# Attention and a spectral filter on one core: how score tiles, fold sums and fillers are planned, and where loads and stores stand

## The chip, the cores and the metric

The kernel runs on one core of a Trainium2 chip. The metric is the device time of one execution in microseconds. Five engines work side by side, each through its own instruction stream: TensorE (PE), VectorE (DVE), ScalarE (ACT), GpSimd (POOL) and SyncE (SP, which only issues transfers here). They wait for each other by semaphores.

## The reference

Two independent results stand side by side in the output, each 2048 x 448:

```
qkv = (x @ wqkv) -> 3 x 16 heads x 2048 x 28
p   = softmax(q k^T / sqrt(28));   a = (p v) @ wo
X   = rfft2(B_x) * (w_r + i w_i);  b = irfft2(X)
out = concat([a, b], -1)
```

The left half is full attention with 16 heads of 28 columns. The right half multiplies a two-dimensional real Fourier transform by given weights and transforms back. All inputs and the output are bf16.

## The kernel before

**Attention.** The 16 heads are four groups (`NG`) of four heads, which share the four row or column quarters of the TensorE array. A *block* is one group with 512 queries: 16 blocks. A block has 16 key chunks of 128 keys. A *unit* is the score tile of one head for one key chunk and 512 queries; there are 16 x 16 x 4 = 1024. A *fill* (`fill`, line 897 on) multiplies up to four units of different heads at once into PSUM banks (line 905). Units go one of two ways. Those of ScalarE are exponentiated in one instruction for one, two or three banks (line 934) into `ET`, which has `ESL = 16` slots. Those of VectorE (key chunks `DKS = (3, 7, 11)`) take a cheaper form: one pass reads the bank, adds a bias and writes 16-bit integers (line 944), whose bits are read as bf16; three shifted copies follow (line 949), and each copy is multiplied by values scaled beforehand (`Vs`, line 516). The four together make a good exponential. The value products (line 1001) of one block add up in one fixed bank, number 6, one step for a ScalarE chunk and four for a VectorE chunk. When the block is closed, `finish` copies the bank out (line 1060), brings the sums of the softmax to lanes with a small product, takes the reciprocal, spreads it with a second product and multiplies on VectorE (line 1058).

**Spectral half.** Rows are folded into even and odd sums (`fold_chunk`, two chunks on VectorE and two on GpSimd, all operations recorded by `tt`, line 546), then come `s_job` and `x_job` (transforms as products with tables), `zmul` (sixteen small operations per tile on GpSimd), `i_job` (back), `combine` (GpSimd) and 16 `y_job` output products. The weights arrive by 16 plain loads and 16 gathers.

**Order.** All streams are written out ahead by a planner in Python with its own clock (`Prog`, and the main loop at the end). ScalarE is served first: a fill is emitted `TH` before ScalarE runs out. Value products, projections and spectral jobs fill the rest in the order of due times (`due`), counted in ScalarE units done. Every instruction has a price; a step of a job is priced by the job's width, even where its product is narrower. Where the plan leaves TensorE idle for more than `FGAP` and its recent activity is below `FACT = 0.95`, a filler is emitted: matmuls of constants into a free bank (line 1333), whose results are not read. VectorE and GpSimd operations that use the port to the on-chip memory that these two share carry `port=True`: such an operation waits for the other engine's last one, so they take turns. Transfers are issued mostly by SyncE, in program order; a transfer's wait holds all transfers behind it.

**Ends.** At the start all of A's input is loaded at once, 20 warm-up matmuls run (line 1089), weights are spread into padded copies (line 424), and the first keys and queries are projected. At the end each output tile goes through one of four staging slots (`astg`) to one store by SyncE (line 761).

Of the kernel before, what the change touches and what calls it, by code (L numbers as in the profile page):

```python
# [13 lines left out]
TAIL = {"pe": 0.28, "act": 0.34, "dve": 0.14, "pool": 0.12, "sp": 0.1}  # L14
# [7 lines left out]
class Prog:  # L22

    def __init__(self, nc, sems):
# [14 lines left out]
        self.port = (None, None, 0.0)  # L39
        self.hist = {e: {} for e in ENG}  # L40
# [51 lines left out]
    def ready(self, eng, reads=(), writes=()):  # L92
        t = 0.0
        for k in list(reads) + list(writes):
            w = self.tw.get(k)
            if w is not None and not (eng == "pe" and w[0] == "pe"):
                t = max(t, w[1])
        for k in writes:
            for r, e in self.tr.get(k, {}).items():
                if r != eng:  # L100
                    t = max(t, e)
        return t
# [19 lines left out]
    def dma(self, eng, fn, sem, reads=(), writes=(), kb=128, issue=0.6):  # L122
        assert not self.blocked((), writes), (eng, reads, writes)
        self._emit_waits(eng, reads, writes)
# [4 lines left out]
        start = max(self.free[eng], self.ready("dma", reads, writes))  # L129
        self.free[eng] = start + issue  # L130
        self.dma_free = max(self.dma_free, start + issue) + kb / 220.0
        self._mark("dma", ev, reads, writes, self.dma_free + 2.0)
# [45 lines left out]
    def flush(self, now):  # L178
        nxt = INF
        again = True  # L180
        while again:
            again = False
            nxt = INF
            for eng in ("dve", "pool"):
# [5 lines left out]
                for n in self.queue[eng]:  # L190
# [45 lines left out]
def spectral_constants():  # L236

    i = np.arange(512)
    even = 2 * np.pi * ((i[:, None] * i[None, :]) % 1024) / 1024
    odd = np.pi * ((i[:, None] * (2 * i[None, :] + 1)) % 2048) / 1024  # L240
# [3 lines left out]
    fo[1, 0, :] = -((-1.0) ** i)  # L244
    tab = np.stack([fe, fo, go]).reshape(3, 2, 4, 128, 512).transpose(0, 3, 1, 2, 4)
    alt = np.zeros((128, 512))
    alt[0] = (-1.0) ** i
    vec = np.zeros((128, 6))
    a = (-1.0) ** np.arange(128)
    vec[:, 0], vec[:, 1], vec[:, 2], vec[:, 3], vec[:, 4], vec[:, 5] = a, a, -a, a, a, -a  # L250
# [5 lines left out]
    t1 = np.zeros((128, 2, 2, KD))  # L256
    for b, m in enumerate((c[0:113], c[113:225], sn[1:113], sn[113:224])):
        t1[0:m.shape[0], b // 2, b % 2] = m
    dd = np.arange(D)
# [12 lines left out]
DKS = (3, 7, 11)  # L272
ND = len(DKS)
ESL = 16
TSL = 8
# [3 lines left out]
FILLER, FGAP, FACT = True, 0.15, 0.95  # L279
DBL, NDF = 2.5, 1  # L280
PH = ((0.10, 0.30), (0.31, 0.44), (0.58, 0.76), (0.78, 0.985))
FOLD = ((0, "pool"), (1, "dve"), (2, "pool"), (3, "dve"))
# [14 lines left out]
def build_kernel(nc, A_x, A_wqkv, A_wo, B_x, B_w_r, B_w_i, out):  # L297
    WARM = 20
# [13 lines left out]
    t1_h = nc.inline_tensor(t1.reshape(128, 4 * KD).astype(bf16np), name="cst_t1")  # L312
    t2_h = nc.inline_tensor(t2.reshape(128, 4 * D).astype(bf16np), name="cst_t2")
    pp = np.arange(128)
    idx = np.zeros((128, 16), np.int32)
    for a in range(2):
        for c in range(4):
            idx[:, 4 * a + c] = np.minimum(1024 * (a + 1) - 128 * c - pp, S - 1)
    for t in range(8):
        idx[:, 8 + t] = np.minimum(2048 - (t // 4) - 256 * (t % 4) - 2 * pp, S - 1)  # L320
    idx[0, 8] = 1024
# [4 lines left out]
    with ctx:  # L326
        sem_names = ["pe", "act", "dve", "pool"]
        sem_names += ["d_x%d" % i for i in range(4)] + ["d_w", "d_wv", "d_wo", "d_c", "d_t", "d_xe"]
        sem_names += ["d_i"] + ["d_xr%d" % i for i in range(4)] + ["d_wr%d" % i for i in range(8)]
        sem_names += ["d_xb%d" % i for i in range(4)] + ["d_f%d" % i for i in range(2)] + ["d_wb%d" % i for i in range(8)] + ["d_o%d" % i for i in range(4)]  # L330
# [7 lines left out]
        wq = sb("wq", [128, 4, NG, 128])  # L338
        wk = sb("wk", [128, 4, NG, 128])
        wo = sb("wo", [128, NG, 448])  # L340
# [3 lines left out]
        Vs = sb("Vs", [128, 2, ND, NW - 1, 128])  # L344
        ET = sb("ET", [128, ESL, 512])
        TT = sb("TT", [128, NW, TSL, 512], I16)
# [3 lines left out]
        cid = sb("cid", [128, 260])  # L350
        R1a = sb("R1a", [128, 7200])
        R1b = sb("R1b", [128, 7616])
        R2 = sb("R2", [128, 8192])
        FR = sb("FR", [128, 2, 4096])
        alt_t = sb("alt", [128, 518])
        T1 = sb("T1", [128, 2, 2, KD])
        T2 = sb("T2", [128, 2, 2, D])
        ptmp = sb("ptmp", [128, 1800], F32)
        idx_t = sb("idx", [128, 16], mybir.dt.int32)
        ext = sb("ext", [128, 2, KD])  # L360
        PS = ctx.enter_context(nc.psum_tensor("PS", [128, 4096], F32))
        ACC = PS[:, 3072:3584]

        wflat = wst[:, :, :].rearrange("p c k -> p (c k)")
        astg = wflat[:, 0:1792].rearrange("p (s d) -> p s d", s=4)
        xB = R1a[:, :].rearrange("p (a c d) -> p a c d", a=4, c=4)
        XZ = R1a[:, :].rearrange("p (t v k) -> p t v k", t=8, v=4)
        fA = R1b[:, 0:7168].rearrange("p (a c d) -> p a c d", a=4, c=4)
        xtra = R1b[:, 7168:7616]
        Wn = R1b[:, 0:7200].rearrange("p (t v k) -> p t v k", t=8, v=4)  # L370
# [3 lines left out]
        Sd = R2[:, :].rearrange("p (b r k) -> p b r k", b=4, r=2)  # L374
# [3 lines left out]
        vec_r = alt_t[:, 512:518].rearrange("p (v k) -> p v k", v=3)  # L378
        onf = onrm[:, :, :].rearrange("p g k -> p (g k)").bitcast(F32)
        LD = onf[:, 1024:3712].rearrange("p (a d) -> p a d", a=6)  # L380
        L0 = {"dve": LD[:, 0:4], "pool": ptmp[:, 0:1792].rearrange("p (a d) -> p a d", a=4)}
# [200 lines left out]
        def s_job(h, r, b, due):  # L582
# [16 lines left out]
            def after():  # L599
                done.add(("s", h, r, b))  # L600
                if all(x in done for x in alls):
                    load_f(2, 1)
                    for t in range(8):
                        load_w(t)
# [792 lines left out]
```

## Time and profile before

| what | value |
|---|---|
| median of 3 runs | 468.45 us (467.98 to 470.62) |
| span of the profiled execution | 460.5 us |
| the median beyond that span | 7.95 us |
| PE busy | 424.8 us, 92% |
| ACT busy | 395.2 us, 86% |
| DVE busy | 348.2 us, 76% |
| POOL busy | 165.5 us, 36% |
| mean granted TensorE clock | 0.978 |

The profile is of one execution and gives its span, from the first instruction to the last; its own device time is not given beside it, so the difference of the median to the span is what lies around. Busy shares are averages over parts with different limits, so the table by stage is the one to read. PEclk is the granted share of TensorE's full clock.

### The profile page before, as it was taken

The page shows a single profiled execution, that of the slowest core. Times are in us where ns is not written, and L with a number is a line of the kernel's source. Part 1 is how long each engine was busy: PE and PEld are TensorE (multiplying, and loading weights), DVE is VectorE, ACT ScalarE, POOL GpSimd, SP SyncE. Part 2 cuts the span into 40 slices and gives each one's busy share as a digit, 9 for nine tenths or more (in the row PEclk, how much of TensorE's full clock was granted, in tenths as well). Part 3 has the DMA queues.
Part 4 walks back from the last instruction along what each step waited for, and adds up shares of the span by engine and source line. Part 5 has one row for each costly group of instructions (what it writes and reads, how often), then busy time and mean ns, then how long its engine had stood idle before and what let it go on. Part 6 is the DMA issues. An engine that isn't in the chain of part 4 may idle for free.

```text
span 460.5 us, 16944 instructions
## 1 busy us (share of the span) xinstructions
PE 424.8 (92%) x7484; PEld 164.9 (36%) x7484; DVE 348.2 (76%) x731; ACT 395.2 (86%) x383; POOL 165.5 (36%) x203
## 2 busy tenths in 40 slices
PE   7889899988998899998998899999899999999994
PEld 3434433332332233433333333333332332423353
DVE  2856699999989397676768788968668788996361
ACT  2687569999999899995899999999999999999911
POOL 8775700000000000686376566465652335320000
PEclk9999999999999899995899999999999999999998
DMA  8940000000000000720000000000000000011132
GB/s 237 333 152 4 3 2 3 1 4 1 3 1 2 1 4 1 210 48 1 2 3 3 2 3 3 2 3 3 1 3 1 4 1 2 3 33 41 62 113 83
DMA packets 13421, 15.92 MB, mean 35 GB/s; under 512 B 3762, under 2 KB 12212, under 8 KB 12964
## 3 DMA queue, kind: packets, MB, share of 16 engines
q1 hardware_dynamic: 11332, 11.39, 8.0%
q0 software_dynamic: 1088, 2.24, 1.8%
q10 hardware_dynamic: 928, 1.20, 0.9%
q8 instruction: 59, 0.97, 0.9%
q14 instruction: 14, 0.11, 0.1%
HBM read 11.16 MB, written 3.67 MB: 32 GB/s over the span
## 4 chain that ended last, share of the span: by engine, by line
PE 41%; ACT 23%; DVE 16%; POOL 8%; DMA 6%; issue 6%; SPq 0%; DVEq 0%; ACTq 0%; POOLq 0%
ACT ET L934 22%; PE PS L443 13%; PE PS L1001 13%; PE PS L905 13%; DVE TT L944 5%; DVE TT L949 4%; POOL R1b L541 3%; DMA out_dram<-wst 2%; DMA R1a<-in_B_x_dram,idx 2%; DVE onrm L546 2%; PE PS L1333 2%; DMA wst<-in_A_wqkv_dram 2%; POOL ptmp L546 1%; POOL R1b L546 1%; POOL wst L546 1%
## 5 line engine op out<-in xcount | busy, mean ns | idle before, releaser
L934 ACT ACTIVATE ET<-PS 128x1024 bf16<-128x1024 f32 (+2 forms) x373 | 388.6, 1153 | 35.4 <-PE PS L905 33.1
L905 PE MATMUL PS<-qT,kT 28*128 28x512 bf16 x1024 | 149.4, 390 | 13.6 <-ACT ET L934 8.9
L944 DVE TENSOR_SCALAR TT<-PS 128x512 int16<-128x512 f32 x192 | 129.5, 685 | 32.8 <-PE PS L905 31.0
L949 DVE TENSOR_SCALAR TT<-TT 128x1024 int16<-128x1024 int16 x288 | 105.9, 421 | 12.8 <-POOL ptmp L546 11.5
L1001 PE MATMUL PS<-ET,Vaug 128*32 128x512 bf16 x832 | 83.4, 394 | 4.4 <-ACT ET L934 3.6
L905 PEld LDWEIGHTS PS<-qT,kT 28*128 28x128 bf16 x1024 | 36.6, 91 | 120.4 <-ACT ET L934 66.3
L1333 PE MATMUL PS<-cid 128*32 128x256 bf16 x1216 | 56.0, 275 | 3.6 <-DVE qT L495 1.3
L541 POOL DMA_INDIRECT R1b<-in_B_w_r_dram,idx x8 | 8.0, 998 | 130.0 <-DVE R L607 127.9
L1001 PE MATMUL PS<-TT,Vs 128*32 128x512 bf16 x576 | 40.3, 384 | 0.1
L1001 PEld LDWEIGHTS PS<-ET,Vaug 128*32 128x32 bf16 x832 | 21.2, 94 | 48.6 <-issue 32.1
L546 POOL TENSOR_TENSOR ptmp<-ptmp,R1b 128x450 f32<-128x450 f32 x32 | 31.6, 1010 | 14.1 <-DVE TT L949 10.0
L1333 PEld LDWEIGHTS PS<-cid 128*32 128x32 bf16 x1216 | 27.1, 95 | 26.7 <-issue 7.7
L546 POOL TENSOR_TENSOR R<-R1b 113x512 bf16<-113x512 f32 (+3 forms) x16 | 20.0, 1276 | 36.3 <-DVE R1b L707 33.8
L546 POOL TENSOR_TENSOR ptmp<-R1a 128x225 f32<-128x225 bf16 (+2 forms) x36 | 25.1, 716 | 15.7 <-DVE TT L949 12.8
L443 PE MATMUL PS<-T,R 112*32 112x448 bf16 (+4 forms) x512 | 28.0, 323 | 2.1 <-DVE TT L944 1.8
L546 POOL TENSOR_TENSOR ptmp<-ptmp 128x225 f32<-128x225 f32 x32 | 18.1, 582 | 17.2 <-DVE TT L949 9.2
L546 POOL TENSOR_TENSOR R1a<-ptmp 128x225 bf16<-128x225 f32 x32 | 18.0, 581 | 12.7 <-DVE TT L949 11.7
L443 PE MATMUL PS<-FR,R1b 128*32 128x512 bf16 (+3 forms) x256 | 21.6, 397 | 0.8 <-ACT ET L934 0.6
L443 PE MATMUL PS<-FR,R1a 128*32 128x512 bf16 (+2 forms) x256 | 21.1, 383 | 0.3
L1001 PEld LDWEIGHTS PS<-TT,Vs 128*32 128x32 bf16 x576 | 15.4, 98 | 14.6 <-DVE TT L949 1.0
L443 PE MATMUL PS<-wv,xAT 112*32 112x112 bf16 x1024 | 20.5, 219 | 0.0
L443 PE MATMUL PS<-xAT,wk 112*32 112x512 bf16 x240 | 19.2, 382 | 0.9 <-DVE xAT L472 0.9
(84 smaller groups left out, 365.4 us busy)
## 6 DMA issues: line engine op xcount, KB each, us to landing
out_dram<-wst SPq DMA_DIRECT2D x32, 112.0 KB, 1.8
FR<-cst_tab SPq DMA_DIRECT2D x3, 1024.0 KB, 10.7
R<-in_A_x_dram SPq DMA_DIRECT2D x4, 448.0 KB, 8.9
R1a<-in_B_x_dram SPq DMA_DIRECT2D x8, 112.0 KB
wst<-in_A_wqkv_dram ACTq DMA_DIRECT2D x1, 784.0 KB, 7.3
R1b<-in_B_w_r_dram SPq DMA_DIRECT2D x8, 56.2 KB
R1b<-in_B_w_i_dram SPq DMA_DIRECT2D x8, 56.2 KB
T<-cst_t SPq DMA_DIRECT2D x1, 448.0 KB
```

What stands on the lines that cost most here:

```text
L443: ins = e.matmul(out[c:c1], lhsT[:, c:c1], rhs, start=start, stop=stop, tile_position=(0, c))
L541: P.dma("pool", lambda e: e.indirect_dma_start(dst, None, src, bass.IndirectOffsetOnAxis(ap=idx_t[:, col:col + 1], axis=0)), sem, reads=[" ...
L546: P.defer(eng, lambda e: e.tensor_tensor(out, a, b, op), reads=reads, writes=writes, busy=c, allow=allow, port=True, after=after)
L905: ins = e.matmul(bank(bk), kT[32 * j:32 * j + DH, g % 2, 128 * kc:128 * (kc + 1)], qT[32 * j:32 * j + DH, b % QSL, :], start=True, stop=Tr ...
L934: P.op("act", lambda e: e.activation(dst, src, ACT.Exp, scale=ESC), reads=[("B", i) for i in o], writes=[("E", p + k) for k in range(n)], ...
L944: P.defer("dve", lambda e, bk=bk, slot=slot: e.tensor_scalar(TT[:, 0, slot, :], bank(bk), BIAS, 0.0, ALU.add, ALU.max), reads=[("B", bk)], ...
L949: P.defer("dve", lambda e, c=c, slot=slot: e.tensor_scalar(TT[:, c, slot - 1:slot + 1, :], TT[:, 0, slot - 1:slot + 1, :], SHF * c, None, ...
L1001: ins = e.matmul(ACC[32 * j:32 * j + 32, :], lh, rhs, start=first, stop=last, tile_position=(0, 32 * j))
L1333: ins = e.matmul(PS[32 * c:32 * c + 32, 512 * bk + h:512 * bk + h + 256], cid[:, 32 * c:32 * c + 32], cid[:, 0:256], start=True, stop=True ...
```

## The change

It replaces large parts of planner and kernel. In words:

- *Units.* `DKS` becomes `KDS = (2, 6, 10, 14)`, a list of chunks that VectorE *may* take. While the plan is made, `d_pick` gives VectorE a chunk of the present or the next block when its backlog is short; what is left at the end of a block's list goes to ScalarE. Shifted copies are made for four units at a time (2048 elements). `ESL` is 25. Fills with two banks prefer pairs with no free neighbours, and all eight banks are used.
- *Value products.* The accumulator is bank 0 or 7 by turns, and a second block can be open beside the first. Passes of VectorE chunks are single steps.
- *Softmax sums.* For all but the last block they go by transfers through memory and come back as broadcasts; GpSimd multiplies. The last block is normalised in two halves by the former way, and its output products are begun with three groups before it is ready.
- *Projections* read the weights as loaded, without the padded copies. Due times are called ahead (`QKL`).
- *Fillers.* `FACT` is 0.55, `FGAP` 0.1; a filler is forced where activity is under `FMIN = 0.44`, into the open accumulator with zero weights if no bank is free.
- *Planner.* Each step of a job is priced by its own columns. GpSimd port operations yield to a VectorE port operation that is due earlier and soon ready. Several knobs are drawn per 32 units from the seeds in `PLAN`.
- *Spectral half.* Reversed orders are put into the tables, so most gathers become plain loads; three fold chunks on GpSimd and one on VectorE; the half transforms release their weights and products separately; `zmul` has eight operations of 450 elements; `x_job` makes sums and differences by a third, negated table; loads are paced by progress.
- *Ends.* The first tokens, the constants and two slices of 98 KB of weights are loaded first; the first exponentials need 128 keys. Eight staging slots; stores by two queues.

```diff
-DKS = (3, 7, 11)
-ESL = 16
-TSL = 8
+KDS = (2, 6, 10, 14)
+ESL = 25
+NST = 8
+TSL = 12
-FILLER, FGAP, FACT = True, 0.15, 0.95
+FILLER, FGAP, FACT, WIN = True, 0.1, 0.55, 3.4
+FORCE, FMIN = True, 0.44
+FOLDV = (3,)
...
+        def step_cost(n):
+            return max(n / 2340.0, 0.052) + 0.0025
...
-            pe_op(m, f[0] if jb.full else f[1], jb.needs, [("B", bk)], jb.n / 2400.0 + 0.004)
+            n = f[2] if len(f) > 2 else jb.n
+            pe_op(m, f[0] if jb.full else f[1], jb.needs, [("B", bk)], step_cost(n), n / 2400.0)
...
+                if best is not None and best.port and eng == "pool" and self.free["dve"] <= now + PHOLD:
+                    rival = [m for m in self.queue["dve"] if m.port and m.due < best.due and all(x.done for x in m.deps)
+                             and self.ready("dve", m.reads, m.writes) <= now + 0.05]
+                    if rival:
+                        nxt = min(nxt, max(self.free["dve"], now + 0.05))
+                        continue
...
+        def d_pick():
+            if prog() < DST:
+                return None
+            ab = next_a()
+            ab = ab[0] if ab is not None else NB
+            for b in range(min(ab, NB - 1), min(ab + 2, NB)):
+                ks = [k for k in rem[b] if k in KDS]
+                ks = [k for k in ks if keys_ok(b, k)] or ks
+                if ks and 4 * len(rem[b]) >= rules()["dend"] + (DLAST if b == NB - 1 else 0):
+                    return b, ks[-1]
+            return None
...
+                for c in range(1, NW):
+                    P.defer("dve", lambda e, c=c, m=m, s0=s0: e.tensor_scalar(TC[:, c - 1, 4 * m:4 * m + 4, :], T0[:, s0:s0 + 4, :], SHF * c, None, ALU.add),
+                            reads=[("T", k) for k in range(s0, s0 + 4)], writes=[("TC", c, m)], busy=0.60, allow=rules()["copies"], port=True)
...
+            if FORCE and now > 14.0 and activity(now) < FMIN and room >= 0.23 + mode_pen("col") and idle_work(now, 512):
+                continue
...
+                P.defer("pool", lambda e: e.tensor_tensor(onrm[:, g, cs], oaug[:, i, :], onrm[:, g, cs], ALU.mult), reads=[ko] + [("rzb", g, qc, j) for j in range(4)],
+                        writes=[("onrm", g, qc)] + old,
+                        busy=1.25, allow=6.0, port=True, after=after)
```

## Rows read from the trace of the kernel before

**Rows 1.** The page's busy shares
```profile
PE 424.8 (92%) x7484; PEld 164.9 (36%) x7484; DVE 348.2 (76%) x731; ACT 395.2 (86%) x383; POOL 165.5 (36%) x203
```

**Rows 2.** The group of fillers on TensorE
```profile
L1333 PE MATMUL PS<-cid 128*32 128x256 bf16 x1216 | 56.0, 275 | 3.6 <-DVE qT L495 1.3 <-DVE TT L944 0.8 <-DVE R L607 0.5
```

**Rows 3.** Busy us by stage: stretch, length, engines (instructions), PEclk, DMA share, GB/s
```profile
0.00:13.65 13.65, 10.65 (x59) 4.42 (x63) 5.11 (x12) 3.37 (x4) 11.20 (x16) 1.00 0.92 251
13.65:60.00 46.35, 42.08 (x934) 20.63 (x927) 32.80 (x72) 31.35 (x30) 31.61 (x20) 1.00 0.32 107
60.00:210.00 150.00, 138.40 (x2348) 50.14 (x2346) 128.18 (x266) 139.67 (x135) 19.12 (x23) 0.98 0.09 22
210.00:330.00 120.00, 113.08 (x2051) 43.70 (x2048) 91.77 (x200) 113.97 (x110) 70.61 (x110) 0.95 0.01 3
330.00:437.10 107.10, 103.20 (x1681) 35.03 (x1673) 81.81 (x168) 103.58 (x100) 32.97 (x37) 1.00 0.05 16
437.10:460.50 23.40, 17.34 (x440) 11.00 (x436) 8.55 (x15) 3.26 (x7) 0.00 (x0) 0.93 0.29 96
```

**Rows 4.** Timeline of the head: first transposes, first exponentials
```profile
8.40 1.10 PE L460 MATMUL PS<-cid,R 128*112 128x128 bf16 x16
13.65 2.45 ACT L934 ACTIVATE ET<-PS 128x1536 bf16<-128x1536 f32 x2 [0.50 <-PE PS L905]
```

**Rows 5.** ScalarE's groups: all, pairs, triples: busy us, mean ns | idle before, releasers
```profile
L934 ACT ACTIVATE ET<-PS 128x1024 bf16<-128x1024 f32 (+2 forms) x373 | 388.6, 1153 | 35.4 <-PE PS L905 33.1 <-ACT ET L934 0.3
...
L934 ACT ACTIVATE ET<-PS 128x1024 bf16<-128x1024 f32 x243 | 240.5, 1053 | 23.5 <-PE PS L905 22.3 <-ACT ET L934 0.3
L934 ACT ACTIVATE ET<-PS 128x1536 bf16<-128x1536 f32 x108 | 158.9, 1490 | 10.2 <-PE PS L905 9.6
```

**Rows 6.** Timeline at 48 to 64: start us, us, what [idle before <-releaser]
```profile
53.41 4.14 POOL L546 TENSOR_TENSOR R1b<-wst 128x896 bf16<-128x896 f32 x2 [2.69 <-DVE TT L949]
57.76 1.09 DVE L949 TENSOR_SCALAR TT<-TT 128x1024 int16<-128x1024 int16 x3
59.87 0.68 DVE L1060 CAST oaug<-PS 128x512 bf16<-128x512 f32 x1
61.37 3.08 ACT L934 ACTIVATE ET<-PS 128x1024 bf16<-128x1024 f32 x3 [9.08 <-PE PS L905]
```

**Rows 7.** Three us by stage, and timeline, where the clock is low
```profile
210.00:213.00 3.00, 3.00 (x43) 1.27 (x40) 2.00 (x5) 2.05 (x2) 1.47 (x3) 0.50 0.00 0
...
208.73 0.94 PE L443 MATMUL PS<-T,R 113*32 113x225 bf16 x16 [1.84 <-DVE TT L944]
215.21 1.02 ACT L934 ACTIVATE ET<-PS 128x1024 bf16<-128x1024 f32 x1 [0.62 <-PE PS L905]
```

**Rows 8.** VectorE's groups of shares, copies and scaled values
```profile
L944 DVE TENSOR_SCALAR TT<-PS 128x512 int16<-128x512 f32 x192 | 129.5, 685 | 32.8 <-PE PS L905 31.0
L949 DVE TENSOR_SCALAR TT<-TT 128x1024 int16<-128x1024 int16 x288 | 105.9, 421 | 12.8 <-POOL ptmp L546 11.5 <-POOL R L546 0.5
L516 DVE TENSOR_SCALAR Vs<-Vaug 128x128 bf16<-128x128 bf16 x36 | 6.5, 191 | 4.8 <-POOL R1b L546 1.9 <-POOL wst L546 1.5 <-POOL R1a L546 0.8
```

**Rows 9.** Timeline, then chain of waits, at the end
```profile
441.01 0.69 DVE L1058 TENSOR_TENSOR onrm<-oaug,PS 128x512 bf16<-128x512 bf16 x1 [1.04 <-PE PS L1046]
...
450.67 1.77 DMA out_dram<-wst
453.41 3.43 DMA out_dram<-wst
```

**Rows 10.** Timeline of TensorE at 425: score fill, value step, next step
```profile
425.26 0.39 PE L905 MATMUL PS<-qT,kT 28*128 28x512 bf16 x3
425.58 0.40 PE L1001 MATMUL PS<-ET,Vaug 128*32 128x512 bf16 x4
425.81 0.74 PE L443 MATMUL PS<-wo,onrm 128*32 128x448 bf16 x12
```

**Rows 11.** Waits of VectorE: us in total, times, longest
```profile
DVE TT L949 <- POOL ptmp L546: 11.5, 10, 2.7
```

More of the change, by code (lines that the diff above doesn't have):

```diff
@@ L1 @@
+import random
 import numpy as np
@@ L839, in plan_fill @@
         def plan_fill(now):
-            banks = [i for i in (0, 1, 2, 3, 4, 5, 7) if bank_free(i, now)]
-            left = NA - st["ai"]
+            banks = [i for i in range(8) if bank_free(i, now)]
+            left = a_left()
             if left == 0 or not banks:
@@ L852, in plan_fill @@
                     trip = trip or [a, a + 1, a + 2]
-            pair = next(([a, a + 1] for a in banks if a + 1 in banks), None)
+            pair = min(([a, a + 1] for a in banks if a + 1 in banks), key=lambda p: (p[0] - 1 in banks) + (p[1] + 1 in banks), default=None)
+            if pair is None and len(banks) > 1:
+                pair = banks[0:2]
             opts = []
@@ new lines, in pv_cands, with acc_bank, pv_reads @@
+            return r
+        def acc_bank(now):
+            best = (INF, None)
+            for i in (0, 7) if st["pb"] % 2 else (7, 0):
+                if i not in reserved and not P.blocked((), [("B", i)]):
+                    best = min(best, (max(P.ready("pe", (), [("B", i)]), now), i), key=lambda x: x[0])
+            return best
+        def pv_reads(c):
+            kind, qi = c
+            b, kc = (AQ if kind == "A" else DQ)[qi]
+            g = b // 4
+            cc = 0 if kind == "A" else npass.get(qi, 0)
+            if kind == "A":
+                rd = [("E", eslot[4 * qi + j]) for j in range(4)]
+            elif cc == 0:
+                rd = [("T", s) for s in dq[qi].values()]
+            else:
+                rd = [("TC", cc, qi % TCQ)]
+            vk, nk = (("V", g % 2, kc // 4), ("V", g, kc // 4)) if cc == 0 else (("Vs", g % 2, KDS.index(kc)), ("Vs", g, KDS.index(kc)))
+            return rd + [vk], nk
@@ L1080, in run_now @@
-        def run_now(jb, bk, eng):
-            for f in jb.mms(bank(bk)):
-                pe_op("full", f[0], jb.needs, [("B", bk)], jb.n / 2400.0 * 2)
-            jb.end(bank(bk), ("B", bk), eng)
-            if eng != "act":
-                while P.queue["dve"]:
-                    P._commit(P.queue["dve"][0])
-        for i in range(WARM):
-            pe_op("full", lambda e: e.matmul(bank(7), onrm[:, 3, 1536:1664], onrm[:, 3, 1536:2048], start=True, stop=True), ["zero"], [("B", 7)], 0.35)
@@ L1169, in job_start @@
                 return None
-            bks = [i for i in (7, 0, 1, 2, 3, 4, 5) if bank_free(i, now)]
+            if jb.bank is not None:
+                return jb.bank
+            if jb.cond is not None and not jb.cond():
+                return None
+            bks = sorted([i for i in range(8) if bank_free(i, now)], key=lambda i: sum(bank_free(i + s, now) if 0 <= i + s < 8 else 0 for s in (-1, 1)))
             return bks[0] if bks else None
```

1085 lines of the change are left out of this document (662 added, 423 removed).

## The prediction

> **What bounds the kernel now.** Start with the page's busy shares [rows 1]: TensorE 92%, ScalarE 86%, VectorE 76%. The 92% misleads, because some of TensorE's time is matmuls of constants whose result nobody reads: the group of line 1333 is 56.0 us [rows 2], and the warm-up at the start some 7 us. Without both, useful TensorE work is about 424.8 - 56.0 - 7 = 362 us of 460.5.
>
> Next read the table by stage [rows 3]. ScalarE, which does 832 of the 1024 score tiles ("units": 128 keys x 512 queries of one head), works 139.7 of 150, 114.0 of 120 and 103.6 of 107.1 us in the three long stages: it sets the pace there. It is not the pace before 60 us (31.4 of 46.4) nor after 437.1 us (3.3 of 23.4). So the span has three pieces with different limits: a head of 13.65 us until the first exponential [rows 4], a stream of 437.1 - 13.65 = 423.45 us, and a tail of 23.4 us.
>
> The stream splits by ScalarE's groups [rows 5]: 373 instructions, of them 243 pairs, 108 triples and so 22 singles, are 832 units in 388.6 busy us, 0.467 us a unit. Idle before exponentials are 35.4 us, 33.1 of it behind score matmuls; less the 0.50 before the first one, 34.9 lie inside the stream: 388.6 + 34.9 = 423.5, as it should be.
>
> Where is that idle? One gap of 9.08 us ends at 61.37 [rows 6]. Follow it back: the accumulator of block 0 is copied out at 59.87, after the value products of its last VectorE chunk, whose copies run at 57.76, behind two GpSimd fold operations that run from 53.41 to 57.55 (the two engines take turns). Meanwhile the results of block 1 fill the 16 slots, since its products can't begin before that accumulator is free. The first of the two stages it lies in (13.65 to 60) has 46.35 - 31.35 = 15.0 us of idle ScalarE, 60 - (61.37 - 9.08) = 7.7 of it in this gap, so 7.3 beside it. And at 210 the granted clock is 0.5, the 1.2 GHz level [rows 7]; before it fell, TensorE had stood 1.84 us waiting for VectorE (until 208.73). With that clock ScalarE starts a pair every 1.02 + 0.62 = 1.64 us, where a pair has 240.5/243 = 0.99 us over the whole stream. It lasts until about 222, some 13.5 us.
>
> **The change part by part.** Durations are of the profiled execution, span 460.5 us; the median of the runs is 468.45, so 7.95 us are taken to lie around the span, now and after.
>
> *Who computes exponentials.* VectorE had a fixed 3 of 16 key chunks (192 units). Now it may take up to 4 of 16 (256) and the split is decided as the program is planned: it takes a chunk when its backlog is short, and what it doesn't take goes to ScalarE. Each moved unit saves ScalarE 0.467 us. What stops it is VectorE. A unit costs one PSUM read, 129.5/192 = 0.675 us, and shifted copies, now 105.9/288 = 0.368 us for 1024 elements, 1.5 per unit [rows 8]. The copies become 2048 long, 0.75 per unit. The trace has no such copy; its price lies between 0.37 (size free) and 0.74 (all size). The line through the 128- and the 1024-element operations (6.5/36 = 0.18 and 0.368) gives 0.58; I take 0.6. A unit is then 0.675 + 0.45 = 1.13 us (0.95 to 1.23). VectorE's other work is 348.2 - 129.5 - 105.9 = 112.8 us. The normalising multiplies go to GpSimd (15 of 16 blocks at 0.69 [rows 9], -10.4), of two fold chunks one goes there (about -8), memsets and weight spreading go (about -3), scaled values grow from 36 to 48 (+2): some 93. At 236 units VectorE is busy 93 + 267 = 360 of about 404 us, 89%. It has been 128.2 of 150 in the best long stage (85%) at a rationed share, so 89% looks reachable, 95% (256 units) doubtful. I take 236 units (200 to 256): ScalarE 788 x 0.467 = 368.0 us, a gain of 20.6 (3.7 to 29.9).
>
> *Stalls in the stream.* Keys and queries are called ahead of need (up to 12 units on), block 0 goes by key quarter, a second block may be accumulated before the first is closed, either of two banks can be the accumulator, 25 instead of 16 slots for results. These meet the 9.08 us gap and the 7.3 us beside it. The idle-time rule is cut (no filler above 0.55 instead of 0.95 of activity) but fillers are now forced when activity falls under 0.44, also in the open accumulator bank with zero weights: this meets stretches such as 207 to 222, which cost 13.5 x (1 - 0.99/1.64) = 5.4 us. What is late next: TensorE itself. I leave 17 of 34.9 us (8 to 35).
>
> *TensorE's load.* In steady state a score fill takes 0.32 us to the next instruction and a value step 0.23 [rows 10]. More VectorE chunks add three value steps each: 11 x 3 x 0.23 = 7.6. The frequency products are built twice (+64 steps of 225 columns at about 0.1 = 6.4) because signs move into a third table, and the normalising products go (15 x 8 small steps at some 0.06 = -7). Real work 362 + 7 = 369 us of 404: 91%, without fillers. So the fillers' place is eaten up by real work, and that is why the idle left is not zero. *A new way for the softmax sums.* They leave by a store to memory, come back one per lane, and after the reciprocal go out and back again as four broadcasts: four transfers, each bounded by the 1.77 and 3.43 us of the stores [rows 9], 7 to 14 us with the waits between. They sit in SyncE's in-order queue, so paced loads and output stores stand behind them, and VectorE's reciprocal waits for a landing. Hidden, because a block lasts 423/16 = 26 us and two buffers hold the sums; the last block keeps the old way through TensorE. If that cover goes, the next block's copy waits and the accumulator with it: 5 us a block at most, which I don't count.
>
> Real lengths for small products change only the plan's order; I give them nothing by themselves (-2 to +2).
>
> *Spectral half.* GpSimd's products go from sixteen small operations per tile to eight of 450 elements, weights come by 2 gathers rather than 16, and each half starts when its half of the transform is done. GpSimd was busy 70.6 of 120 us at 210 to 330 [rows 3] and the output products came last because of it. This is off the path in the stream (bound: 0), but it lets the 16 output products start before the stream's end, which the tail needs. The third fold chunk (some 12 us) and 15 multiplies of about 1.2 go onto GpSimd, 165.5 us busy now, and are hidden there; if not, the fold delays only work that is due 100 units later.
>
> *Head.* First transposes begin at 8.40 and the first exponential at 13.65 [rows 4]; ahead of 8.40 all 448 + 784 + 392 + 3 x 448 KB are queued at once, at 251 GB/s [rows 3]. Now the first tokens (448 KB), 65 KB of constants and two slices of 98 KB go first, and only 448 KB beside them: 1157 KB at 251 GB/s is 4.6 us, with some 1.5 us until data moves: 6.1 instead of 8.4. The chain after it starts from 128 keys rather than 512, without the spreading of weights: 5.25 us become about 3.4. First exponential at 9.5 (8.5 to 13), a gain of 4.15.
>
> *Tail.* The chain after the last exponential ends with the normalisation at 441.01 + 0.69 [rows 9]; one output product (0.4), eviction 0.62 and a store of 1.77 would end at 444.6, 7.5 us after 437.1. The rest, until 460.5, is 24 output tiles squeezed through four staging slots and one queue: the last waits are for stores (1.77 us at 450.67, 3.43 at 453.41 in the chain of waits). Eight slots, two queues, output products ahead of the end, and the last block normalised in halves take that away; four last tiles leave the chain some 2 us longer. Tail 9.5 (8 to 16), a gain of 13.9.
>
> Sum: head 9.5 + ScalarE 368.0 + idle 17 + tail 9.5 = 404.0; with 7.95 around it 412 us, a gain of 56.5.
>
> **Rivals.**
> *VectorE and GpSimd meet.* The shifted copies waited 11.5 us for GpSimd, ten times, 1.15 each [rows 11], and these two take turns by order of the program. With copies longer and more operations on GpSimd, if half of 59 chunks meet one, the loss is 30 x 1.15 = 34 instead of 11.5 us: 23 us of VectorE, 20 units fewer, 9.4 us. With 200 units it is 17 us: 421 to 429. For it: VectorE has no slack at 89%; against: fewer, longer copies meet less often.
> The Trainium skill, SBUF — State Buffer, "SBUF: two separate sides", says the port pair of the two engines is an exclusive lock held for a whole instruction, the other one blocked in full. By that rule alone longer copies and more GpSimd work cost what the waits above cost; the row agrees in kind, 11.5 us, and the same 421 would come out.
> *TensorE becomes the bound.* 369 us of real work at 88% use rather than 91% is a span of 419: 427 us. For it: every fill switches the array's tiling; against: 103.2 of 107.1 us at 330 to 437 are busy, fillers included.
> *All goes well.* 256 units (358.7), idle 8: 392 us.
> *Slower: the clock.* If fewer fillers let TensorE drop to 1.2 GHz often, a us there loses 1 - 0.99/1.64 = 0.40 us. The gain is used up once 56.5/0.40 = 141 us of stream run there, ten stretches like 207 to 222. With 160 us it is 476. Against it: with 91% real work, pauses like 1.84 us get rare.
> *It doesn't do what it says.* The plan's clock drifts from the chip's, waits of in-order queues eat the gain: 455 to 466.
>
> **How the numbers follow.** Forecast (400 to 420) 0.55; meeting on the port 0.14; TensorE bound 0.14; all goes well 0.11; little gained 0.03, a third of it within 0.5%; slower by the clock 0.03. The range 394 to 432 leaves out about 2 in 10, its ends from 256 units with some idle and from TensorE bound with a longer tail. About 0.5% is what a measurement here tells from no change: faster 0.96, within 0.01, slower 0.03.
>
> **What would show it.** Right: first exponential near 9.5, ScalarE with about 788 units and under 20 us idle before them, VectorE with about 236 units at about 360 us, the constant matmuls far below 56 us with a clock of 1.0, last exponential some 9.5 us ahead of the end. Wrong: under 210 VectorE units, granted clock 0.5 in several stretches, or a tail that still waits for stores.

## The result and the profile after

| what | before | after |
|---|---|---|
| median, us | 468.22 (466.49 to 470.62, 4 runs) | 401.88 (401.43 to 402.47, 4 runs) |
| ratio, 95% interval | | 0.862 (0.858 to 0.866) |
| span of the profiled execution, us | 460.5 | 400.2 |
| its own time, us | not given | 401.99 |
| first exponential starts, us | 13.65 | 8.66 |
| last exponential ends, us | 437.1 | 391.74 |
| mean granted TensorE clock | 0.978 | 0.991 |

The forecast was 412, with a range of 394 to 432. The spans differ by 60.3 us: 5.0 in the head, 40.4 in the stream of exponentials, 14.9 in the tail.

The page of the changed kernel, busy shares and two lines of its 40 slices (one digit each, busy tenths; PEclk is the granted clock):

```profile
PE 384.3 (96%) x6312; PEld 130.8 (33%) x6312; DVE 331.8 (83%) x599; ACT 382.5 (96%) x394; POOL 155.9 (39%) x144
...
ACT  4999999999999996999999999999999999899993
...
PEclk9999999999999996999999999999999999999999
```

Beside [rows 1], ScalarE went from 86% to 96% of its span with less work. One slice, the sixteenth, stands out in both lines. The table by stage, to be read beside [rows 3] (columns as there):

```profile
0.00:8.66 8.66, 7.03 (x93) 3.52 (x94) 1.95 (x6) 2.75 (x4) 4.46 (x8) 1.00 0.74 203
8.66:60.00 51.34, 50.14 (x978) 20.07 (x978) 39.77 (x83) 51.08 (x52) 24.66 (x21) 1.00 0.28 77
60.00:150.00 90.00, 85.06 (x1276) 26.09 (x1276) 80.08 (x139) 90.00 (x90) 28.53 (x22) 1.00 0.17 47
150.00:165.00 15.00, 13.62 (x160) 3.73 (x160) 10.94 (x18) 11.19 (x11) 6.13 (x6) 0.77 0.01 2
165.00:280.00 115.00, 114.13 (x2036) 40.27 (x2028) 104.77 (x194) 114.85 (x118) 62.80 (x63) 1.00 0.09 23
280.00:391.70 111.70, 108.67 (x1646) 34.36 (x1650) 90.33 (x156) 110.39 (x119) 29.33 (x24) 1.00 0.13 40
391.70:400.20 8.50, 5.62 (x142) 2.78 (x132) 3.94 (x10) 2.21 (x5) 0.00 (x0) 1.00 0.37 123
```

ScalarE (the fourth busy number) is now full from the first exponential on: 51.08 of 51.34 us up to 60, where it had 31.35 of 46.35, and 90.00 of 90.00 behind that. The one large hole is in 150 to 165, 11.19 of 15 us at a mean clock of 0.77. The groups that answer to [rows 5, 8] (busy us, mean ns | idle before, releaser):

```profile
L1178 ACT ACTIVATE ET<-PS 128x1024 bf16<-128x1024 f32 (+2 forms) x386 | 377.5, 1207 | 6.1 <-PE PS L1144 5.7
L1188 DVE TENSOR_SCALAR T<-PS 128x512 int16<-128x512 f32 x200 | 135.1, 686 | 21.6 <-PE PS L1144 20.0
...
L1201 DVE TENSOR_SCALAR TC<-T 128x2048 int16<-128x2048 int16 x150 | 96.9, 686 | 9.7 <-POOL ptmp L627 2.7
...
L1178 ACT ACTIVATE ET<-PS 128x1024 bf16<-128x1024 f32 x248 | 245.0, 1144 | 4.9 <-PE PS L1144 4.6 <-PE PS L509 0.3
L1178 ACT ACTIVATE ET<-PS 128x1536 bf16<-128x1536 f32 x95 | 146.0, 1584 | 1.1 <-PE PS L1144 1.1
L1178 ACT ACTIVATE ET<-PS 128x512 bf16<-128x512 f32 x43 | 26.4, 740 | 0.1
```

The last three lines are the first one's pairs, triples and singles. VectorE took 200 units, so ScalarE has 824, in 377.5 us (0.458 each), and the idle before exponentials fell from 35.4 to 6.1 us; 0.58 of it lies before the first one. The fillers, which had 56.0 us [rows 2], in the groups with the forms kept apart:

```profile
L1002 PE MATMUL PS<-cid 128*32 128x256 bf16 x148 | 6.9, 275 | 0.1
```

With 2.3 us of the other filler form and 3.6 of warm-up, TensorE's real work is 384.3 - 12.8 = 371.5 us.

The hole at 150, in the timeline (start us, us, engine, line, what [idle before <-releaser]):

```profile
143.99 3.09 SPq L1328 DMA_DIRECT2D onrm<-scr  x4
...
148.75 1.15 POOL L1330 TENSOR_TENSOR onrm<-oaug,onrm 128x512 bf16<-128x512 bf16 x1 [4.69 <-DMA onrm<-scr]
...
149.94 0.69 DVE L1201 TENSOR_SCALAR TC<-T 128x2048 int16<-128x2048 int16 x1 [1.93 <-POOL onrm L1330]
...
151.38 0.61 PE L1144 MATMUL PS<-qT,kT 28*128 28x512 bf16 x3 [1.62 <-DVE T L1188]
...
152.03 1.02 ACT L1178 ACTIVATE ET<-PS 128x1024 bf16<-128x1024 f32 x1 [1.54 <-PE PS L1144]
```

Read it downwards, each line the releaser of the next. SyncE issues the four broadcasts of a block's reciprocals in 3.09 us; GpSimd's normalising multiply waits 4.69 us for them, in its turn; a VectorE copy behind that turn waits 1.93; TensorE waits 1.62 for a bank that VectorE has not read; ScalarE waits 1.54. Then the granted clock falls to 0.5, the 1.2 GHz level, and the bill goes on for nearly 7 us, until 158. The first 2 us from 152:

```profile
152.00:154.00 2.00, 2.00 (x18) 0.45 (x22) 1.97 (x4) 1.23 (x2) 0.83 (x1) 0.50 0.03 8
```

TensorE is busy throughout, and ScalarE gets 1.23 of 2 us.

### The profile page after: what moved, and what is told of

It reads as the page before. It is cut to its first block, busy times and chain, and to the rows that moved or that the text cites. A ratio compares the mean times of both kernels' runs of the same rounds, so it can differ in the third digit from the quotient of the medians.

```text
span 400.2 us, 14693 instructions
## 1 busy us (share of the span) xinstructions
PE 384.3 (96%) x6312; PEld 130.8 (33%) x6312; DVE 331.8 (83%) x599; ACT 382.5 (96%) x394; POOL 155.9 (39%) x144
## 4 chain that ended last, share of the span: by engine, by line
ACT 45%; PE 39%; issue 5%; DMA 5%; POOL 2%; DVE 1%; SPq 1%; POOLq 0%; DVEq 0%; ACTq 0%
ACT ET L1178 45%; PE PS L1144 12%; PE PS L469 11%; PE PS L1280 9%; PE PS L509 4%; DMA onrm<-scr 2%; DMA scr<-rz 2%; SPq L1328 1%; DMA R<-in_A_x_dram 1%; POOL onrm L1330 1%; POOL R L627 1%; DVE T L1188 1%; PE PS L1438 0%; PE PS L487 0%; DVE TC L1201 0%
## 5 line engine op out<-in xcount | busy, mean ns | idle before, releaser
L1178 ACT ACTIVATE ET<-PS 128x1024 bf16<-128x1024 f32 (+2 forms) x386 | 377.5, 1207 | 6.1 <-PE PS L1144 5.7
L1188 DVE TENSOR_SCALAR T<-PS 128x512 int16<-128x512 f32 x200 | 135.1, 686 | 21.6 <-PE PS L1144 20.0
L1201 DVE TENSOR_SCALAR TC<-T 128x2048 int16<-128x2048 int16 x150 | 96.9, 686 | 9.7 <-POOL ptmp L627 2.7
L1280 PE MATMUL PS<-TC,Vs 128*32 128x512 bf16 x600 | 53.6, 386 | 0.6 <-DVE TC L1201 0.6
L1330 POOL TENSOR_TENSOR onrm<-oaug,onrm 128x512 bf16<-128x512 bf16 x15 | 17.3, 1156 | 91.5 <-DMA onrm<-scr 59.0
L509 PE MATMUL PS<-xAT,wst 112*28 112x512 bf16 x480 | 38.0, 383 | 0.1
L627 POOL TENSOR_TENSOR R<-R1b 113x512 bf16<-113x512 f32 (+1 forms) x16 | 20.1, 1279 | 24.0 <-DVE R1b L803 21.7
L627 POOL TENSOR_TENSOR ptmp<-R1a,R1b 128x450 f32<-128x450 bf16 x24 | 22.9, 972 | 15.3 <-DVE TC L1201 10.0
L1393 DVE CAST wst<-PS 128x448 bf16<-128x448 f32 x28 | 17.4, 622 | 12.8 <-PE PS L469 11.0
L627 POOL TENSOR_TENSOR ptmp<-ptmp 128x450 f32<-128x450 f32 x16 | 18.1, 1142 | 12.6 <-DVE TC L1201 7.3
L469 PE MATMUL PS<-wv,xAT 112*32 112x112 bf16 x1024 | 21.3, 214 | 0.3 <-DVE xAT L495 0.3
L469 PE MATMUL PS<-T,R 112*32 112x225 bf16 (+2 forms) x520 | 21.0, 264 | 0.0
L1280 PE MATMUL PS<-T,Vaug 128*32 128x512 bf16 x200 | 19.8, 386 | 0.0
L1280 PEld LDWEIGHTS PS<-TC,Vs 128*32 128x32 bf16 x600 | 13.7, 95 | 17.4 <-issue 8.4
```

The source lines that it names most:

```text
L469: ins = e.matmul(out[c:c1], lhsT[:, c:c1], rhs, start=start, stop=stop, tile_position=(0, c))
L509: ins = e.matmul(M[32 * j:32 * j + DH], wst[0:112, c, off + DH * j:off + DH * j + DH], xAT[0:112, c, 512 * n:512 * (n + 1)], start=c == 0, ...
L627: P.defer(eng, lambda e: e.tensor_tensor(out, a, b, op), reads=reads, writes=writes, busy=c, allow=allow, port=True, after=after)
L1178: P.op("act", lambda e: e.activation(dst, src, ACT.Exp, scale=ESC), reads=[("B", i) for i in o], writes=[("E", p + k) for k in range(n)], ...
L1188: P.defer("dve", lambda e, bk=bk, slot=slot: e.tensor_scalar(T0[:, slot, :], bank(bk), BIAS, 0.0, ALU.add, ALU.max), reads=[("B", bk)], wr ...
L1201: P.defer("dve", lambda e, c=c, m=m, s0=s0: e.tensor_scalar(TC[:, c - 1, 4 * m:4 * m + 4, :], T0[:, s0:s0 + 4, :], SHF * c, None, ALU.add) ...
```

## The experiments

Each was timed in four runs, beside runs of the kernel before. The medians of before in the three series were 464.41, 465.09 and 464.36, with single executions from 457.41 to 470.43, so kernels built from the changed one are compared with the changed kernel, which holds between 401.06 and 402.96 in all its runs, and ratios are to the before of the same series. The changed kernel was timed for the result and in the first series alone. What is compared with it from the seeds on is compared across series, whose medians of before differ by 0.7 us.

**The changed kernel once more.** No edit.

> The changed kernel again, as the mark for the three beside it and for the time around the span. Theory 1: the 7.95 us around the span of the kernel before was a difference between one quick profiled execution and the median, so here too the time is about 1.8 us above the span: 400 to 403. Theory 2: the change itself shortened what lies around the span: then kernels before show 6 to 8 us and this one 1.8, in every run.

401.87 us (401.06 to 402.96), ratio 0.869 (0.862 to 0.877); span 400.2. In each of its executions the time is 1.8 us above the span. The same holds for before: in the executions run beside it and in the later series, 22 in all, the time lies 1.8 to 2.0 us above the span, for example 464.44 at 462.6. The 7.95 us of the forecast were never around the span.

**Fillers cut to one column.** Same plan and same count of instructions.

```diff
-ins = e.matmul(PS[..., 512 * b + h:512 * b + h + 256], ..., cid[:, 0:256], ...)
+ins = e.matmul(PS[..., 512 * b + h:512 * b + h + 1], ..., cid[:, 0:1], ...)
```

> The changed kernel with the same plan, each filler matmul cut to one column. Theory (real work alone holds the clock): granted clock 0.97 or more, at most one stretch at 0.5 beyond the one at 151 to 158, time 400 to 406. Rival (the 44 us less of fillers were bought by placing the few that are left well): three or more new stretches at 0.5 of 7 to 13 us, each costing 40% of its length, time 408 to 418.

411.98 us (409.14 to 413.21), 10.1 more. The fillers' 9.2 us of TensorE time are worth as much in ScalarE's pace: its idle time doubles (6.1 to 11.9 us in the profiled execution, the shortest of the four), and one stretch of the window table shows why.

```profile
100.00:108.00 8.00, 8.00 (x74) 1.52 (x71) 5.01 (x9) 6.22 (x7) 3.37 (x3) 0.53 0.08 16
```

Full use of TensorE, a granted clock of 0.53, and ScalarE busy 6.22 of 8 us; in the changed kernel this stretch is part of the 90.00 of 90.00.

**The normalising multiply out of the turns.** GpSimd's multiply of line 1330 neither waits for VectorE's last port operation nor holds up VectorE's next. The edit reaches further than that: the planner keeps only the last port operation, so a GpSimd operation right behind the multiply doesn't wait for VectorE either.

```diff
-... if port and self.port[0] not in (None, eng) else None)
+... if port is True and self.port[0] not in (None, eng) else None)
...
-            self.port = (eng, ev, start + busy + TAIL[eng])
+            self.port = (eng, ev if port is True else None, start + busy + TAIL[eng])
...
-                        busy=1.25, allow=6.0, port=True, after=after)
+                        busy=1.25, allow=6.0, port="quiet", after=after)
```

> The changed kernel with the same plan, but the 15 normalising multiplies of GpSimd take no part in the turns with VectorE, so no copy waits for one that itself waits for its broadcasts. Theory (the late broadcasts at 149 stop VectorE's copies, then TensorE, then the clock): the gap of 1.54 us at 150 and the stretch at 0.5 behind it go, ScalarE's idle time falls from 6.1 to under 3 us, time 3 to 5 us less: 397 to 399. Rival (something else is late there as well): within 1 us of the changed kernel.

404.34 us (402.12 to 408.9), no gain, where 397 to 399 was expected. The hole at 150 is gone (ScalarE busy 6.00 of 6 and 8.00 of 8 us from 146 to 160, clock 1.00), which shows that the turn behind a late broadcast made it. But another opens at 312, in the timeline of this kernel:

```profile
308.31 1.16 POOL L1330 TENSOR_TENSOR onrm<-oaug,onrm 128x512 bf16<-128x512 bf16 x1
...
308.46 4.91 DVE L1201 TENSOR_SCALAR TC<-T 128x2048 int16<-128x2048 int16 x3 [0.19 <-POOL R L627]
...
309.43 3.39 POOL L627 TENSOR_TENSOR R<-R1b 113x512 bf16<-113x512 f32 x2
...
314.62 1.45 ACT L1178 ACTIVATE ET<-PS 128x1536 bf16<-128x1536 f32 x1 [2.50 <-PE PS L1144]
```

Three copies take 4.91 us while GpSimd works; in the changed kernel three such copies take 1.90 us near the same place. Only the first of the copies meets the multiply; the others meet the two fold operations (line 627) behind it, which wait for no semaphore here. So this loss belongs to the edit's reach, and what the multiply alone would gain out of the turns stays open. ScalarE then waits 2.50 us, and the clock is 0.61 from 315 to 319.

**No turns at all.** VectorE and GpSimd no longer wait for each other at the port; only the waits for data are left.

```diff
-        self._emit_waits(eng, reads, writes, self.port[1] if port and self.port[0] not in (None, eng) else None)
+        self._emit_waits(eng, reads, writes)
```

> The changed kernel with the same plan and no turns at all between VectorE and GpSimd: neither waits by semaphore for the other's port operation. Theory (turns guard VectorE: without them its copies meet GpSimd's operations and stretch): mean copy rises from 0.69 to 0.8 us or more, VectorE late, time 404 to 410. Rival (turns only add waits): copies stay within 0.05 us, GpSimd's waits of some 90 us for VectorE vanish, time 396 to 400.

459.06 us (453.11 to 464.75): 57 us more by the medians, 51 for its shortest run: most of the gain, and many times what was expected. The profile is of the longest of these runs. The copies, in the view of one tile (ns min/median/max, first and last start), in the changed kernel:

```profile
L1201 DVE TENSOR_SCALAR TC<-T x150: 628/686/695, 29.6 to 375.7; 128x2048 int16<-128x2048 int16 x150
```

and without turns:

```profile
L1201 DVE TENSOR_SCALAR TC<-T x150: 627/685/2578, 36.6 to 438.0; 128x2048 int16<-128x2048 int16 x150
```

ScalarE's group in the kernel without turns:

```profile
L1178 ACT ACTIVATE ET<-PS 128x1024 bf16<-128x1024 f32 (+2 forms) x386 | 385.5, 1149 | 60.7 <-PE PS L1144 59.9 <-PE PS L509 0.3
```

The instructions are the same, and so is the median copy, but 38 of the 150 take more than 800 ns, the longest 2578 instead of 695, and the mean goes from 686 to 876 ns, as that theory said: the wait now sits inside the instruction, at moments that no plan chose. VectorE's busy time rises from 331.8 to 380.4 us, TensorE waits for its banks, the clock falls (0.77 from 230 to 300) and ScalarE idles 60.7 us.

**Seeds off.** The knobs that are drawn per 32 units keep their defaults.

```diff
-                p = PLAN[k] != 0
+                p = False
```

> The changed kernel with no seeds: one fixed set of knobs in all stretches. VectorE's units stay 200. Theory (the idle time went by structure: slots, second open block, look-ahead, turns): ScalarE's idle time rises from 6 to at most 14 us, time 404 to 411. Rival (it went by choosing among plans): idle time 25 us or more, time above 420.

406.93 us (404.76 to 408.11), 5 more. ScalarE's group:

```profile
L1178 ACT ACTIVATE ET<-PS 128x1024 bf16<-128x1024 f32 (+2 forms) x377 | 377.4, 1211 | 6.2 <-PE PS L1144 5.6 <-ACT ET L1178 0.3
```

and, in the table by stage, the stretch behind the last exponential:

```profile
391.37:405.20 13.83, 10.71 (x248) 5.85 (x240) 6.20 (x13) 3.80 (x7) 0.00 (x0) 0.97 0.38 128
```

Busy and idle time of ScalarE are those of the changed kernel. The 5 us stand in the tail, 13.83 against 8.46: with the seeds, TensorE has 142 matmuls left there instead of 248.

**One open block and 16 result slots**, as the kernel before has them.

```diff
-ESL = 25
+ESL = 16
...
-            for b in range(st["pb"], min(st["pb"] + (2 if ("blk", st["pb"]) in done else 1), NB)):
+            for b in range(st["pb"], min(st["pb"] + 1, NB)):
```

> The changed kernel with 16 result slots and one open block, as before the change, seeds kept; VectorE then has 204 units. Theory (slots and the second block took away the waits at the ends of blocks, as at 52 to 61 of the kernel before): ScalarE's idle time rises by 15 to 25 us, most of it in gaps of over 1 us near the ends of blocks, time 416 to 430. Rival (look-ahead and pricing did): below 410.

418.31 us (417.83 to 419.37), 16.4 more, at a clock of 1.0: a stall that owes nothing to the clock. Two gaps in ScalarE's timeline carry 14 of its 25.0 us of idle time:

```profile
337.01 45.15 ACT L1178 ACTIVATE ET<-PS 128x1536 bf16<-128x1536 f32 x44 [7.59 <-PE PS L1144]
...
388.62 20.45 ACT L1178 ACTIVATE ET<-PS 128x1536 bf16<-128x1536 f32 x18 [6.46 <-PE PS L1144]
```

They are of the kind of the 9.08 us gap of before [rows 6]: in each, the accumulator is copied out (at 335.43 and 387.66) and ScalarE goes on 1.0 to 1.6 us later.

**16 result slots alone**, the second open block kept.

```diff
-ESL = 25
+ESL = 16
```

> The changed kernel with 16 result slots, but a second open block allowed; seeds kept, VectorE then has 204 units. Together with the run that had neither (418.3 us, idle 25.0): if the slots alone do it, 414 to 419 and idle 20 us or more; if the second open block does it, 402 to 408 and idle under 12 us.

403.47 us (401.83 to 404.85), with 10.0 us of idle ScalarE, 5.09 of it in one gap that ends at 333.79. So with 16 slots the second open block is worth 418.31 - 403.47 = 14.8 us (both plans give VectorE 204 units). With the second block open, the nine slots are worth some 1.6, which the runs' scatter does not tell from nothing. One open block with 25 slots was not run: whether slots alone would have done much of the same stays open.

**Steps priced by the job's width**, as before, with the seeds off; to be compared with the seeds-off kernel.

```diff
-            n = f[2] if len(f) > 2 else jb.n
+            n = jb.n
```

> Seeds off as in the run beside it, and each step of a job priced by the job's width again rather than by its own columns. Theory (real lengths let small products fit into short gaps): 2 to 6 us more than with seeds off alone. Rival (pricing only changes order): within 2 us of it, either way.

411.83 us (408.92 to 415.91), 4.9 above the seeds-off kernel. The profiled execution is the longest of the four; its ScalarE idles 10.9 us instead of 6.2. Of the 8.9 us between the two profiled spans, 5.0 stand in the tail: 18.85 us with 356 matmuls left, where the seeds-off kernel has 13.83 with 248. This is one pair of plans, and the seeds alone move a plan by 5 us in the same place. That the real lengths matter, and not just another order, is not shown.

**VectorE held to 2 of 16 chunks**, seeds off.

```diff
-KDS = (2, 6, 10, 14)
+KDS = (6, 14)
```

> Seeds off, and only 2 of 16 key chunks open to VectorE: 120 instead of 200 units. Theory (ScalarE sets the pace, one unit 0.458 us): 80 x 0.458 = 37 us more than with seeds off alone, less some 4 us of idle time that is left: 30 to 37 more, about 437 to 447. Rival (TensorE at 96% is as much the bound, and a unit moved back saves it 0.17 us): only 15 to 25 us more.

428.24 us (427.92 to 429.25), 21.3 above the seeds-off kernel, for 80 units moved back to ScalarE. The rival's 15 to 25 came, not the theory's 30 to 37:

```profile
L1178 ACT ACTIVATE ET<-PS 128x1536 bf16<-128x1536 f32 (+2 forms) x365 | 410.0, 1351 | 3.1 <-PE PS L1144 3.0
```

ScalarE's busy time rises by 32.6 us, 0.41 a unit since more of them come in triples (189 instead of 102). TensorE, with 240 value steps fewer, gives some back: the tail is 6.85 us (80 matmuls left) instead of 13.83 (248) and the idle time 3.1 less. Net, a moved unit is worth 21.3/80 = 0.27 us.

**The kernel before with fillers of one column.**

```diff
-ins = e.matmul(PS[..., 512 * bk + h:512 * bk + h + 256], ..., cid[:, 0:256], ...)
+ins = e.matmul(PS[..., 512 * bk + h:512 * bk + h + 1], ..., cid[:, 0:1], ...)
```

> The kernel before with the same plan, each filler matmul cut to one column. Theory (its real work, 362 of 460 us, can't hold the clock alone): granted clock under 0.9, ScalarE's idle time well above the 35 us of before, time 485 or more. Rival (fillers there were mostly waste, as the change's thin use of them suggests): within 5 us of the kernel before.

492.01 us (488.56 to 494.02), ratio 1.066 (1.054 to 1.078): the 56.0 us of fillers hold off some 28 us by the medians, 30 by the ratio. ScalarE's group in this kernel:

```profile
L934 ACT ACTIVATE ET<-PS 128x1024 bf16<-128x1024 f32 (+2 forms) x373 | 391.0, 1137 | 61.8 <-PE PS L905 58.9 <-ACT ET L934 0.3
```

Its idle time is 61.8 us where the kernel before has 35.4 [rows 5], at a mean clock of 0.87.

**The kernel before with eight staging slots.**

```diff
-        astg = wflat[:, 0:1792].rearrange("p (s d) -> p s d", s=4)
+        astg = wflat[:, 0:3584].rearrange("p (s d) -> p s d", s=8)
...
-                slot = oct_[0] % 4
+                slot = oct_[0] % 8
```

> The kernel before with eight staging slots for output tiles instead of four, nothing else. Theory (the tail of 23.4 us waits for stores): the tail shrinks by 4 to 9 us, the time with it. Rival (the 24 tiles that are left after the last exponential set it, by TensorE and eviction): within 2 us.

456.64 us (455.78 to 458.17), ratio 0.991 (0.981 to 1.001). By the times alone this is unclear, since before scatters; the profile shows where it went. The stretch behind the last exponential:

```profile
437.50:454.80 17.30, 13.66 (x312) 7.79 (x308) 8.83 (x15) 3.26 (x6) 0.00 (x0) 1.00 0.39 129
```

17.3 us where it was 23.4 [rows 3]; the stream ends where it did. In that stretch of before, ScalarE and VectorE together wait 13.7 us for a staging slot's last store; with eight slots neither does.

**A real price for the broadcasts.** The changed kernel issues a block's four broadcasts in 1.71 to 3.09 us and its planner has them at 4 x 0.1. Here they are priced 0.5 each, and the seeds are drawn anew, because the old ones belong to the old plan.

```diff
-                          ... writes=[("rzb", g, qc, j)] + (old if j == 0 else []), kb=32, issue=0.1)
+                          ... writes=[("rzb", g, qc, j)] + (old if j == 0 else []), kb=32, issue=0.5)
```

> The changed kernel with the four broadcasts of the softmax sums priced in the plan at 0.5 us of issue each, about what SyncE needs in the trace (3.09 us for four with a wait in it), instead of 0.1, and seeds chosen anew for that plan. Theory (the multiply is planned too early, VectorE's copies wait their turn behind it, TensorE stops and the clock falls): no stretch at 0.5 in the stream, ScalarE's idle time under 4 us, 397 to 400.5. Rival (another order brings another stall of that size): 401 to 404.

398.02 us (396.63 to 399.71), ratio 0.863 (0.854 to 0.872) to its own series; 3.9 below the changed kernel, and each of its runs is below each run of that one. ScalarE's group:

```profile
L1178 ACT ACTIVATE ET<-PS 128x1024 bf16<-128x1024 f32 (+2 forms) x371 | 376.1, 1236 | 1.1 <-PE PS L1144 0.6 <-PE PS L509 0.3
```

and the whole stream as one stretch of the table by stage:

```profile
8.35:385.10 376.75, 366.12 (x6036) 123.32 (x6040) 324.36 (x583) 376.15 (x372) 150.28 (x136) 1.00 0.13 40
```

The hole at 150 is gone, and with it any other: 376.15 of 376.75 us. How much of the 3.9 us the price gives and how much the new seeds was not taken apart.

## Why the prediction came out as it did

| term, us | predicted | measured | error |
|---|---|---|---|
| head | 9.5 | 8.66 | -0.8 |
| ScalarE busy | 368.0 (788 units x 0.467) | 377.5 (824 x 0.458) | +9.5 |
| idle in the stream | 17 | 5.5 | -11.5 |
| tail | 9.5 | 8.46 | -1.0 |
| around the span | 7.95 | 1.8 | -6.2 |
| sum | 412 | 402.0 | -10.0 |

Two errors of some 10 us lie inside the span and nearly cancel, by luck: 404.0 was forecast for it and 400.2 came. What moved the total besides is a term with no mechanism behind it.

**The step that failed is the one on the execution's own time**: "the median of the runs is 468.45, so 7.95 us are taken to lie around the span". Around the span lie 1.8 us in both kernels (the changed kernel once more). So the profiled execution of before took about 460.5 + 1.8 = 462.3 us, and its median execution is longer inside the span, not around it: before spreads, in one series from 457.68 us at a mean clock of 0.994 to 469.38 at 0.963. The forecast's own gain, 56.5, stands against 460.5 - 400.2 = 60.3 in spans and 66.3 between the medians. Had 1.8 been used, the sum would have been 405.8.

**Units.** VectorE took 200, not 236, and so the sign that was named for a wrong forecast, under 210, came true. The price of a unit was nearly right: 0.675 for the read and 0.75 x 0.646 for copies make 1.16 us against 1.13, and VectorE's other work is 331.8 - 135.1 - 96.9 = 99.8 us against 93. The copy alone was set too low at 0.6: it takes 96.9/150 = 0.646 us busy and 686 ns by itself. (The Trainium skill, VectorE: DVE Perf Modes, "The perf-mode tier table (the rule you actually need)", states 693 ns for a `tensor_scalar` on 2048 bf16 elements in SBUF. This trace agrees with 686 for its 16-bit integers.) But VectorE is 83% busy, not 89: it did not fill up. Nor does the port stop it: the idle time before its copies is 9.7 us in all, 12.8 before [rows 8]. The number is fixed when the program is planned: 200 in the plans without seeds, with the old step prices and with the new broadcast price too, 204 in those with 16 slots. So some rule or price of the plan keeps it there; which one stays open. That its reads wait 20.0 us for score fills, and that TensorE is at 96%, is a hint and no more.

**Moved work is not worth its price.** The 0.467 us a unit was the gross price. With 80 units moved it is 0.27 net (VectorE held to 2 of 16). The drop from 388.6 to 377.5 us is, by the arithmetic of the groups, 8 units x 0.467 = 3.7 and 824 x 0.009 = 7.4 from a lower price of each unit, which the forecast did not have. The lower price is not the mix, which got worse: 95 triples and 43 singles, where before has 108 and 22 among its 373. It is the same idle time once more. A pair that begins behind an idle ScalarE takes 1.02 us (the line at 152.03), and eight pairs in a row end 0.917 us apart:

```profile
142.97 7.52 ACT L1178 ACTIVATE ET<-PS 128x1024 bf16<-128x1024 f32 x8
```

Singles, pairs and triples alike cost some 0.107 us less where they begin before the last one has ended. Behind the first, 75 exponentials of before begin only when the last one has ended, and 10 of the changed kernel: 65 x 0.107 = 7.0 of the 7.4 us.

**Idle.** This is the main gain, 34.9 to 5.5 us, and it was mis-sized in the other direction: 17 were left because TensorE was thought to come late next. Two of the mechanisms named are shown. One open block and 16 slots put the idle time at 25.0 us again, and with 16 slots the second open block is worth 14.8 us of time. So a stall like block 0's [rows 6] goes when the next block need not wait for the accumulator; whether more slots alone would have done it was not run. The 10 us between 25.0 and before's 34.9 (calling ahead, block 0 by key quarter, forced fillers) were not taken apart. The clock's part [rows 7] is real too: without fillers' columns the changed kernel loses 10 us, before loses some 28.

**TensorE.** Its real work was forecast at 369 us and is 371.5, but it fits into 400.2 us: 93%, more than the 91 assumed and far from the 88 of that rival. 427 was refuted by the run itself. The nearness is in part luck: with the 200 units that VectorE took, the forecast's own terms give 362 + 1.4 + 6.4 - 7 = 363. The rival in which all goes well adds up to 393.7, not to the 392 that it names.

**The port rival** (421 to 429) did not come, though its 200 units did. It had the copies wait 34 us for GpSimd in their turns, and they wait at most 9.7. What the turns hold off is something else, which the forecast did not price: without them 57 us go. The Trainium skill, SBUF — State Buffer, "SBUF: two separate sides", calls the pair an exclusive lock in which the other engine blocks in full; the copies of up to 2578 ns agree. By that rule alone the turns would gain nothing, since either way one engine waits. The runs show that they do gain; that the planner can plan round a turn and cannot round a lock is a reading that fits them, argued and not shown.

**Priced at nothing.** Real lengths were given -2 to +2 us; the one pair of plans that differs in them differs by 4.9, with the seeds off. The broadcasts through memory were called hidden, 5 us a block if not; for one of the 15 blocks they were late and made the one large hole of the stream, some 4 us (11.19 of 15 in that stretch). The seeds were not in the sum at all: 5 us, in the tail.

**Head and tail** were right within some 1 us. No run takes the head's 5.0 us apart. Of the 14.9 us of the tail, eight slots give 6.1 in the kernel before; what the two queues, the halves of the last block and the early output products give each was not tried.

So the head, the tail and the kind of each gain were read rightly from the profile, the sizes of the two largest terms were not, and that their errors had opposite signs was luck.

## What to carry to other kernels

Check what lies around the span on an execution that has both numbers before adding a median to a profile: a difference of medians and span may be a quicker execution. Where a fast engine sets the pace, look first for what empties its supply (here one accumulator that had to close before the next opened, 14.8 us with 16 slots) and only then for work to take off it, and price that net (0.27 us, not 0.467). In an order that is written out ahead, an underpriced queue instruction can open a hole, as it did in one block of 15: with four small transfers at nearer their real issue time, and seeds drawn for that plan, nearly all the idle time that was left went.

## What the runs showed of the hardware

- Where VectorE's copies and GpSimd's operations take no turns, single copies stretch (38 of 150 over 800 ns, 2578 at the longest, 695 with turns; the median stays at 685), and their records show it as busy time, not as a wait: 125.7 us busy and 0.1 idle before them, with turns 96.9 and 9.7. Taking turns by semaphores is worth 57 us in this kernel.
- An exponential that begins before the one ahead has ended costs ScalarE some 0.107 us less than one that begins behind an idle engine (0.917 against 1.023 us for a pair, by the medians of both traces). So an idle ScalarE costs more than the idle time.
- A single wait of 1.62 us of TensorE at 150 was followed by nearly 7 us at a granted clock of 0.5, in which TensorE was busy from 151.38 on. Cutting the matmuls whose results nobody reads to one column, 9.2 us of them, made the changed kernel 10 us longer, and 56.0 us of them the kernel before some 28.
- Four broadcasts of 32 KB take SyncE 1.71 to 3.09 us to issue: 0.42 each by the median, and 1.64 for one of those in front of the hole at 150.
